# Strassen's method for both feed-forward products of a windowed attention block

## The chip, the cores and the metric

The kernel runs on one core of a Trainium2 chip. A core has five engines with queues of their own: TensorE (PE: matmuls, and PEld for their weight loads), VectorE (DVE), ScalarE (ACT), GpSimd (POOL) and SyncE (SP), which issues the DMAs here. Each engine works its queue in order. Matmuls write into PSUM (eight banks of 128 x 512 floats); everything else lies in SBUF. The metric is the device time of one execution in microseconds.

## The reference

```python
def _attn_ref(q, k, v):                      # q, k, v: 8 x 8 heads x 576 x 64
    scores = scale * np.matmul(q, k.transpose(0, 1, 3, 2))
    rel = pos[:, None] - pos[None, :]
    mask_plain = (rel >= 0) & (rel < 32)                           # heads 0 to 3
    mask_dil = (rel >= 0) & (rel < 128) & (rel % 4 == 0)           # heads 4 to 7
    scores = np.where(masks, scores, -1e9)
    attn = np.exp(scores - np.max(scores, axis=-1, keepdims=True))
    return np.matmul(attn / (np.sum(attn, axis=-1, keepdims=True) + 1e-09), v)

def _moe_ref(x, g_ln, w_ch1, w_ch2):         # x: 8 x 576 x 512, w_ch1: 512 x 2048
    mu, var = np.mean(x, -1, keepdims=True), np.mean((x - mu) ** 2, -1, keepdims=True)
    xn = (x - mu) / np.sqrt(var + 1e-06) * g_ln
    return x + np.maximum(xn @ w_ch1, 0.0) @ w_ch2
```

Attention with a window of 32 keys (plain or with a stride of 4), then a normalisation, a product with a 512 x 2048 weight, a relu, a product with a 2048 x 512 weight, and the residual sum. The rows, 8 x 576, are 36 tiles of 128.

## The kernel before

Each tile of 128 rows goes through the same stages. Its queries, keys and values are loaded (`L` in the program's table of units). TensorE makes the scores (`S`, L196) of the window in PSUM; VectorE adds the mask (L204) and takes the maximum (L213), GpSimd subtracts it (L225), ScalarE takes the exponential (L226), VectorE transposes (L228): `M`. TensorE multiplies with the values (`V`, L250), VectorE divides (L255 to L260) and four DMAs put the strided heads into the rows `x` (L267). `N` normalises: L274 to L278 on VectorE, the power on GpSimd (L279, `rstd`), `xn` on VectorE (L288). `xn` is then written as two float16 halves, the upper by a cast on ScalarE (`xh`, L293), the lower by a subtraction on GpSimd (`xl`, L294), and two transposing DMAs (`T`, L301) bring both into the layout that the matmuls need.

Both weights, too, are kept as two float16 halves, so that a float32 product is three float16 matmuls: upper with upper, upper with lower, lower with upper. In the first 100 us both weights are unpacked, scaled and split, mostly by VectorE (L386 to L391 and L137).

The feed-forward part works on blocks of three tiles. An "up" product takes 12 matmuls of 384 columns for each of 16 slices of 128 hidden units (L322); ScalarE writes the relu's upper half (`hh`, L328) and VectorE the lower one (`hl`, L329). A "down" product of one tile takes 48 matmuls of 512 columns (L345); VectorE scales it and adds `x` (L351), and a DMA writes the tile out. In the first two blocks, six tiles, the up products go tile by tile, with 128 columns.

The order of the work comes from a table of units with due times and predecessors; they are emitted in the order of these times, and a scheduler that keeps a timeline of its own then places every engine's instructions.

## Time and profile before

| | before |
|---|---|
| median of 3 runs | 926.09 us (924.34 to 927.63) |
| profiled execution: time, span | 925.45 us, 923.70 us |
| granted TensorE clock, mean | 0.985 |
| TensorE busy | 872.5 us, 94% |
| weight loads (PEld) busy | 518.8 us, 56% |
| VectorE busy | 364.3 us, 39% |
| ScalarE busy | 179.8 us, 19% |
| GpSimd busy | 102.3 us, 11% |
| DMA | 75.33 MB, mean 82 GB/s |

A row of instruction groups reads: line, engine, operation, output and inputs with their shapes, count | busy time in us, mean ns of one | idle time of the engine just before them, and who ended it. A row of the chain of waits reads: start, length in us, and what it was; the chain is followed back from the last instruction to whatever released each step. A row of the timeline reads: start, length, engine, line, operation, and in brackets the idle time before it. Matmuls are pipelined, so the length of one is longer than its share of a stream.

### The profile page before, as it was taken

To read this page: it belongs to the slowest core of one execution; us is meant where nothing else is said; L and a number is where in the kernel's file an instruction comes from. 1 tells how busy PE (TensorE), PEld (TensorE's weight loads), DVE (VectorE), ACT (ScalarE), POOL (GpSimd) and SP (SyncE) were. 2 spreads that over 40 slices of the span, in tenths; PEclk is the share of its full clock that TensorE was granted. 3 is DMA by queue.
4 is the path that set the end of the run, shared out by engine and by line. 5 is a ranking of instruction groups with operands and counts; after the bars stand their busy time and mean duration, and the time that the engine had idled before them with its cause. 6 is when DMAs were issued, how large, how long until landed. Compare 5 with 4: busy or idle time off the path is not lost.

```text
span 923.7 us, 27029 instructions
## 1 busy us (share of the span) xinstructions
PE 872.5 (94%) x12392; PEld 518.8 (56%) x12392; DVE 364.3 (39%) x727; ACT 179.8 (19%) x332; POOL 102.3 (11%) x125
## 2 busy tenths in 40 slices
PE   3459999999999999999999999999999999999998
PEld 2358575767554654654654554554554554554553
DVE  5998622334432432432432432432432432340220
ACT  4464410111210210210210210220220120120210
POOL 1011211111111111111101101101101111110000
PEclk9968999999999999999999999999999999999999
DMA  9963322432222221321312312322212212110000
GB/s 326 345 234 98 71 70 72 109 76 71 82 59 81 71 59 55 97 60 51 99 46 65 98 39 68 93 56 70 77 54 73 80 52 69 37 24 29 12 1 35
DMA packets 95154, 75.33 MB, mean 82 GB/s; under 512 B 44800, under 2 KB 77120, under 8 KB 95040
## 3 DMA queue, kind: packets, MB, share of 16 engines
q1 hardware_dynamic: 95040, 73.60, 27.0%
q8 instruction: 97, 1.59, 0.7%
q14 instruction: 17, 0.14, 0.0%
HBM read 49.97 MB, written 9.44 MB: 64 GB/s over the span
## 4 chain that ended last, share of the span: by engine, by line
PE 81%; SPq 2%; DVE 2%; DMA 1%; issue 1%; ACT 1%; POOL 0%; DVEq 0%; POOLq 0%; ACTq 0%
PE ps_f L345 38%; PE ps_f L322 36%; PE ps_v L250 4%; PE ps_s L196 3%; DMA x<-xd 1%; SPq L267 1%; SPq L301 1%; DVE bs L274 0%; SPq L158 0%; DVE hl L329 0%; ACT xh L293 0%; DVE xn L288 0%; ACT hh L328 0%; POOL rstd L279 0%; DVE row L351 0%
## 5 line engine op out<-in xcount | busy, mean ns | idle before, releaser
L345 PE MATMUL ps_f<-w_sb,hh 128*128 128x512 f16 x1152 | 343.0, 379 | 2.0 <-ACT hh L328 2.0
L322 PEld LDWEIGHTS <-w_sb 128*128 128x128 f16 x3072 | 255.8, 99 | 129.7 <-issue 2.8
L345 PE MATMUL ps_f<-w_sb,hl 128*128 128x512 f16 x576 | 218.3, 379 | 1.6 <-DVE hl L329 1.5
L322 PE MATMUL ps_f<-xT,w_sb 128*128 128x384 f16 (+1 forms) x1536 | 199.0, 292 | 14.9 <-DMA xT<-xh 12.6
L322 PE MATMUL ps_f<-w_sb 128*128 128x384 f16 (+1 forms) x1536 | 193.3, 286 | 0.0
L345 PEld LDWEIGHTS <-hh 128*128 128x128 f16 x1152 | 109.9, 98 | 130.4 <-ACT hh L328 2.3
L329 DVE SCALAR_TENSOR_TENSOR hl<-ps_f,hh 128x384 f16<-128x384 f32 (+1 forms) x184 | 104.7, 572 | 189.5 <-ACT hh L328 189.4
L328 ACT ACTIVATE hh<-ps_f 128x384 f16<-128x384 f32 (+1 forms) x184 | 91.6, 502 | 323.1 <-PE ps_f L322 323.1
L345 PEld LDWEIGHTS <-hl 128*128 128x128 f16 x576 | 56.4, 98 | 70.0 <-DVE hl L329 2.4
L279 POOL TENSOR_TENSOR rstd<-rstd,mhalf 128x1 f32<-128x1 f32 x36 | 21.8, 605 | 540.9 <-DVE rstd L278 530.3
L293 ACT CAST xh<-xn 128x512 f16<-128x512 f32 x36 | 22.2, 618 | 233.0 <-DVE xn L288 233.0
L351 DVE SCALAR_TENSOR_TENSOR row<-ps_f,s,x 128x512 f32<-128x512 f32 x36 | 27.0, 750 | 97.7 <-PE ps_f L345 97.7
L274 DVE BATCH_NORM_STATS2 bs<-x 128x6 f32<-128x512 f32 x36 | 24.9, 692 | 91.4 <-DMA x<-xd 91.4
L250 PE MATMUL ps_v<-vs,pt 32*32 32x65 f32 x3328 | 54.4, 228 | 0.0
L294 POOL TENSOR_TENSOR xl<-xn,xh 128x512 f16<-128x512 f32 x36 | 43.7, 1213 | 57.9 <-ACT xh L293 50.7
L250 PE MATMUL ps_v<-v_prev,pt 32*32 32x65 f32 x1152 | 48.4, 229 | 0.5 <-DVE pt L228 0.5
L225 POOL TENSOR_TENSOR sc<-sc,mx 128x512 f32<-128x512 f32 x32 | 34.3, 1072 | 122.6 <-DVE mx L213 109.2
L250 PEld LDWEIGHTS ps_v<-vs,pt 32*32 32x32 f32 x3328 | 46.4, 105 | 0.7 <-issue 0.7
L196 PE MATMUL ps_s<-ks,q 64*32 64x64 f32 (+1 forms) x2976 | 42.0, 218 | 3.6 <-issue 3.6
L196 PEld LDWEIGHTS ps_s<-ks,q 64*32 64x32 f32 x2976 | 34.6, 109 | 18.6 <-issue 18.1
L250 PEld LDWEIGHTS ps_v<-v_prev,pt 32*32 32x32 f32 x1152 | 38.0, 105 | 12.2 <-issue 11.0
L226 ACT ACTIVATE p<-sc 128x512 f32<-128x512 f32 x32 | 20.2, 630 | 116.3 <-POOL sc L225 116.3
(49 smaller groups left out, 313.1 us busy)
## 6 DMA issues: line engine op xcount, KB each, us to landing
slot<-in_w SPq DMA_DIRECT2D x14, 1024.0 KB, 7.7
ks<-in_qkv SPq DMA_DIRECT2D x36, 256.0 KB, 3.3
q<-in_qkv SPq DMA_DIRECT2D x36, 256.0 KB, 3.5
vs<-in_qkv SPq DMA_DIRECT2D x36, 256.0 KB, 3.8
out_x<-row SPq DMA_DIRECT2D x36, 256.0 KB, 2.0
x<-xd SPq DMA_DIRECT2D x144, 32.0 KB, 2.1
v_prev<-in_qkv SPq DMA_DIRECT2D x35, 128.0 KB, 3.0
slot<-in_w SPq DMA_DIRECT2D x4, 512.0 KB, 8.0
```

Source lines behind the costliest of these rows:

```text
L196: nc.tensor.matmul(sc[pj, b, h, cols], q[on, h, pj], keys, start=not early and n == 0, stop=not early and n == len(terms) - 1 or early and ...
L225: nc.gpsimd.tensor_tensor(out=sc, in0=sc, in1=mx.broadcast_to([P, 2, HP, 2 * W]), op=ALU.subtract)
L250: nc.tensor.matmul(pv[to, b, g, e], pt[pj, b, h, n], v[pj, f, e], start=n == 0 or b == 1 and old is None, stop=n == 1,)
L274: nc.vector.bn_stats(bs, x)
L279: nc.gpsimd.tensor_tensor(out=rstd, in0=rstd, in1=mhalf, op=ALU.pow)
L293: nc.scalar.copy(xh, xn)
L294: nc.gpsimd.tensor_tensor(out=xl, in0=xn, in1=xh, op=ALU.subtract)
L322: nc.tensor.matmul(z[:, n], l, r, start=(m == 0), stop=(m == len(mm) - 1))
L328: nc.scalar.activation(hh, z, AF.Relu)
L329: nc.vector.scalar_tensor_tensor(out=hl, in0=z, scalar=0.0, in1=hh, op0=ALU.max, op1=ALU.subtract)
L345: nc.tensor.matmul(o, l, r, start=(f == 0 and m == 0), stop=(f == NFC - 1 and m == 2))
L351: nc.vector.scalar_tensor_tensor(out=y, in0=o, scalar=state["inv"], in1=state[t]["x"], op0=ALU.mult, op1=ALU.add,)
```

## The change

Tiles 0 to 5 keep the plain products, now always tile by tile. From tile 6 on, tiles go in pairs, 256 rows. Both operands of a product are cut into quarters, and in place of eight products of quarters there are seven, on sums of quarters (the form with 15 additions). The first weight's columns and the second's rows are cut into two hidden halves of 1024 (`s` = 0 and 1), and each half of a pair has seven up products (`U`, 24 matmuls of 128 columns each, L418 of the new file) and seven down products (`D`, 12 matmuls of 256 columns each, L487). The constant `ORDER` lists one pair's work: `U04` is up, half 0, product 4; `N01` and `N05` are the next pair's `U01` and `U05`; `S0`, `S1`, `V0` and `V1` are scores and values of the first and second tile of pairs to come.

- Sums of the weights, `T1` to `T4` for each weight and each fourth of the hidden units, are made once and kept: `T1` and `T2` on GpSimd, `T3` and `T4` on VectorE, each with a cast on ScalarE (L390 to L400). `T4` overwrites a quarter and waits for the last plain product that reads it.
- `norm` of a pair's second tile makes four sums of quarters on GpSimd (L300) and then the halves of five quarters, 1280 columns, in one cast (L308) and one subtraction (L309); its two transposing DMAs carry 1280 columns. The transposed operand of a pair has one buffer.
- Partial sums stay in PSUM: products 1, 6, 7 and 4 accumulate in one bank, 5 and 3 in another, and between them the running sum is copied out (L435, ScalarE) or added up (L440, VectorE). Relu, four more sums of the hidden quarters (L445, VectorE), a cast on ScalarE (L426) and a subtraction on GpSimd (L427) make the halves of seven operands, `A11`, `A12`, `A22` and `S1` to `S4`, per hidden half.
- Each of the 14 down products of a pair is added into `x` in place (L498, VectorE), and `x` itself is written out.
- Scores and values share two PSUM banks; six are left for products.

```diff
-NB = 3
+FIRST = 6
+KQ = 256
...
-        xh = work.tile([P, DM], F16, name="xh")
-        xl = work.tile([P, DM], F16, name="xl")
-        nc.scalar.copy(xh, xn)
-        nc.gpsimd.tensor_tensor(out=xl, in0=xn, in1=xh, op=ALU.subtract)
...
+            for to, x0, x1, op in ((4, 2, 3, add), (5, 4, 0, sub), (1, 1, 5, sub), (2, 0, 2, sub)):
+                nc.gpsimd.tensor_tensor(out=xs[:, to], in0=xs[:, x0], in1=xs[:, x1], op=op)
+            st.update(halves_for_transpose(xs[:, 1:6], 1))
...
+    def combine(w, op, fg):
+        sub, add = ALU.subtract, ALU.add
+        x, y = {"T1": ("12", "11"), "T2": ("22", None), "T3": ("22", "12"), "T4": ("21", "T2")}[op]
+        e = nc.vector if op in ("T3", "T4") else nc.gpsimd
...
+    PRODUCTS = {
+        1: ("A11", "11"), 2: ("A12", "21"), 3: ("S4", "22"), 4: ("A22", "T4"), 5: ("S1", "T1"), 6: ("S2", "T2"),
+        7: ("S3", "T3"),
+    }
...
+    def up_product(n, s, to, start):
+        x, w = PRODUCTS[n]
+        q = QUARTER[x]
+        for j in range(HG):
+            fc = slice(j % 2 * P, (j % 2 + 1) * P)
+            ws = piece(0, w, 2 * s + j // 2)
+            for k in range(2):
+                for m, (l, r) in enumerate(triple([a[:, k, fc] for a in ws], (xT_pair[:, 0, q, k], xT_pair[:, 1, q, k]))):
+                    nc.tensor.matmul(
+                        to[:, j * P : (j + 1) * P], l, r, start=start and j == 0 and k == 0 and m == 0,
+                        stop=j == HG - 1 and k == 1 and m == 2, skip_group_check=not start,
+                    )
+
+    def halves(name, me, z):
+        h = me[name] = halves_tile()
+        hh, hl = flat(h)
+        nc.scalar.copy(hh, z)
+        nc.gpsimd.tensor_tensor(out=hl, in0=z, in1=hh, op=ALU.subtract)
+
+    def up(n, s, t0):
...
+        def added(x, z, name):
+            with tc.high_priority():
+                nc.vector.tensor_tensor(out=z, in0=x, in1=z, op=ALU.add)
+            nc.scalar.activation(z, z, AF.Relu)
+            halves(name, me, z)
+
+        def summed(to, x, y, op, name):
+            nc.vector.tensor_tensor(out=me[to], in0=me[x], in1=me[y], op=op)
+            halves(name, me, me[to])
...
+        else:
+            up_product(4, s, me["u"], False)
+            me["z21"] = f32_tile()
+            with tc.high_priority():
+                nc.scalar.activation(me["z21"], me["u"], AF.Relu)
+            me["s"] = f32_tile()
+            summed("s", "z21", "z22", ALU.add, "S1")
+            summed("z21", "z11", "z21", ALU.subtract, "S3")
+            summed("z11", "s", "z11", ALU.subtract, "S2")
+            summed("z12", "z12", "z11", ALU.subtract, "S4")
...
+        def to_x(i, half, ps):
+            x = state[t0 + i]["x"][:, half * KQ : (half + 1) * KQ]
+            with tc.high_priority():
                 nc.vector.scalar_tensor_tensor(
...
+                    out=x, in0=ps[:, 0:KQ], scalar=state["inv"], in1=x, op0=ALU.mult, op1=ALU.add
                 )
...
+        bank_of, adds = {
+            1: ("du", ((0, 0),)), 5: ("df", ((1, 1),)), 6: ("du", ((0, 1),)), 2: ("de", ((0, 0),)),
+            3: ("df", ((0, 1),)), 7: ("du", ((1, 1),)), 4: ("du", ((1, 0),)),
+        }[n]
...
+    ORDER = (
+        "U06", "U02", "V0", "U03", "U07", "S1", "U11", "U15", "U04", "U16", "U12", "U13", "U17", "D01", "D05", "V1", "U14", "D06",
+        "D02", "D03", "D07", "S0", "D11", "D15", "D04", "D16", "D12", "D13", "D17", "N01", "N05", "D14",
+    )
```

What the scheduler makes of it is seen in the engines' queues. GpSimd before, in the steady part, has three instructions a tile (`sc` is the subtraction before the exponential):

```order
L225 TENSOR_TENSOR sc<-sc,mx 128x512
L279 TENSOR_TENSOR rstd<-rstd,mhalf 128x1
L294 TENSOR_TENSOR xl<-xn,xh 128x512
L225 TENSOR_TENSOR sc<-sc,mx 128x512
L279 TENSOR_TENSOR rstd<-rstd,mhalf 128x1
```

and now, from the last lower half (`h`, L427) of the three made of products 2, 3 and 7 of half 0 to the second tile's `xl`:

```order
L427 TENSOR_TENSOR h<-z,h 128x512
L309 TENSOR_TENSOR xl_13664<-xs,xh_13663 128x512
L222 TENSOR_TENSOR sc<-sc,mx 128x512
L427 TENSOR_TENSOR h<-z,h 128x512 x11
L276 TENSOR_TENSOR rstd<-rstd,mhalf 128x1
L300 TENSOR_TENSOR xs<-xs 128x256 x4
L222 TENSOR_TENSOR sc<-sc,mx 128x512
L309 TENSOR_TENSOR xl_14078<-xs,xh_14077 128x1280
```

The second tile's `rstd` has moved behind eleven lower halves; in some pairs one of these comes behind it, and `sc` between the four sums.

VectorE at the same place, from the statistics of the second tile (L271) on, with `z` for sums of hidden quarters and `ps_f` for products:

```order
L271 BN_STATS bs_6841<-x_6761 128x6
L445 TENSOR_TENSOR z_6468<-z_6795,z_6468 128x512
L498 SCALAR_TENSOR_TENSOR x_5412<-ps_f_6660,s2_1703,x_5412 128x256
L273 BN_AGGR mv_6843<-bs_6841 128x2
L445 TENSOR_TENSOR z_6570<-z_6570,z_6468 128x512
L275 TENSOR_SCALAR rstd_6845<-mv_6843 128x1
L498 SCALAR_TENSOR_TENSOR x_5412<-ps_f_6827,s2_1703,x_5412 128x256
L498 SCALAR_TENSOR_TENSOR x_5412<-ps_f_6679,s2_1703,x_5412 128x256
L290 TENSOR_SCALAR xs_6437<-x_6761,mv_6843,rstd_6845 128x512
L498 SCALAR_TENSOR_TENSOR x_5848<-ps_f_6660,s2_1703,x_5848 128x256
L201 TENSOR_TENSOR sc_6920<-ps_a_6883,mask_16_75 128x512
L210 TENSOR_REDUCE mx_6938<-sc_6920 128x8
```

The normalising instruction (L290) waits for GpSimd's `rstd`, and additions into `x` and the next scores stand behind it. In the weight stage, VectorE's queue has sums of `T3` between the splits of the first weight (L133) and the unpacking of the second (L537):

```order
L133 SCALAR_TENSOR_TENSOR w_sb<-w_sb,gs 128x512 x2
L397 TENSOR_TENSOR z<-z,w_sb 128x512
L133 SCALAR_TENSOR_TENSOR w_sb<-w_sb,gs 128x512
L395 TENSOR_TENSOR z<-w_sb 128x512
L537 SCALAR_TENSOR_TENSOR w_sb<-w_sums 128x1024 x2
L257 TENSOR_TENSOR x<-ps_a,rs 128x256
```

where before only splits and unpacking stood; sixteen instructions of `T3` come before the second weight's scale.

More of the change, by code (lines that the diff above doesn't have):

```diff
@@ L167, in slot @@
     def slot():
-        return work.tile([P, CW * DM * 2], I32, name="slot", bufs=SLOTS)
+        n = state["raws"] = state.get("raws", -1) + 1
+        return w_sums[:, 1 + n % 5].rearrange("p c f -> p (c f)").bitcast(I32)
     def attn_scores(t):
@@ L213, in attn_softmax @@
         nc.vector.reduce_max(mx, sc, axis=AX.X)
[L214 removed]
+        p32 = work.tile([P, 2, HP, 2 * W], F32, name="sc") if t < EARLY else sc
         by = 1.0 / 8.0
@@ new lines, in transposes, with bank, triple @@
+    def transposes(t):
+        st = state[t]
+        for a, src in enumerate((st["xh"], st["xl"])):
+            if t < FIRST:
+                out_ = x_place(t)[:, a]
+            else:
+                i = (t - FIRST) % 2
+                out_ = xT_pair[:, a, 2 * i : 2 + 5 * i].rearrange("p q k n -> p (q k) n")
+            nc.sync.dma_start_transpose(out=out_, in_=src)
+    def bank():
+        return ps_f.tile([P, DM], F32, name="ps_f")
+    def triple(w, x):
+        (wh, wl), (xh, xl) = w, x
+        return (wh, xh), (wh, xl), (wl, xh)
@@ new lines, in piece @@
+    def piece(w, name, fg):
+        half = slice(0, 2) if name in ("11", "12") else slice(2, 4)
+        cols = slice(0, KQ) if name in ("11", "21") else slice(KQ, 2 * KQ)
+        if name[0] == "T":
+            n = int(name[1])
+            if n < 4:
+                return [sums_16[:, 3 * w + n - 1, fg, :, a] for a in range(2)]
+            half, cols = slice(0, 2), slice(KQ, 2 * KQ)
+        if w == 0:
+            return [w1_16[:, fg, half, a, cols] for a in range(2)]
+        return [w2_16[:, 4 * fg + half.start : 4 * fg + half.stop, a, cols] for a in range(2)]
@@ new lines, in down_product @@
+    def down_product(n, s, to, start, me):
+        x, w = PRODUCTS[n]
+        h = me[x]
+        for j in range(HG):
+            wh, wl = (a[:, j % 2] for a in piece(1, w, 2 * s + j // 2))
+            hh, hl = h[:, 0, j], h[:, 1, j]
+            for m, (l, r) in enumerate(((hh, wh), (hh, wl), (hl, wh))):
+                nc.tensor.matmul(
+                    to[:, 0:KQ], l, r, start=start and j == 0 and m == 0,
+                    stop=j == HG - 1 and m == 2, skip_group_check=not start,
+                )
@@ L370, in to_f32 @@
+        start = n in (1, 5, 2)
+        if start:
+            me[bank_of] = bank()
+        down_product(n, s, me[bank_of], start, me)
+        for i, half in adds:
+            to_x(i, half, me[bank_of])
+        if s == 1 and n in (3, 4):
+            t = t0 + (n == 4)
+            nc.sync.dma_start(out=out[t * P : (t + 1) * P, :], in_=state[t]["x"])
     def to_f32(src, dst, ps, weights, start, stop, first=False):
@@ L418, in prep_w1 @@
         fs = slice(fg * DM, (fg + 1) * DM)
-        wf = w1_sb[:, fg + 1]
-        ps = ps_f.tile([P, DM], F32, name="ps_f")
+        wf = w1_f32(fg)
+        ps = bank()
         for c in range(0, NKC, CW):
@@ L437, in load_w2 @@
         if f == 0:
-            state["w2_ps"] = ps_f.tile([P, DM], F32, name="ps_f")
+            state["w2_ps"] = bank()
         to_f32(
@@ new lines, in attention_then_ffn @@
+    base, at, step = start + 2 * TOOK["U"], {}, 0.0
+    for what in ORDER:
+        at[what] = step
+        step += TOOK[what[0]]
+    products = []
+    for t in range(FIRST, NT, 2):
+        now = base + step * ((t - FIRST) // 2)
+        for what in ORDER:
+            kind = what[0]
+            if kind in "UD":
+                products.append((now + at[what], kind, t, int(what[1]), int(what[2])))
+            elif kind == "N" and t + 2 < NT:
+                products.append((now + at[what], "U", t + 2, 0, int(what[2])))
@@ new lines, in attention_of_pair @@
+    def attention_of_pair(t0, last_up):
+        for i in range(2):
+            t, now = t0 + i, base + step * ((t0 - FIRST) // 2)
+            s, v = now - step * (2 - i) + at[f"S{i}"], now - step + at[f"V{i}"]
+            attention(t, s, s + SOFTMAX, v, v + NORM, v + NORM + READY, last_up)
+    attention_of_pair(FIRST, f"U{FIRST - 1}.3")
+    for n in (1, 5):
+        products.append((start + 0.3 * n, "U", FIRST, 0, n))
+    was = f"D{FIRST - 1}.3"
+    for when, kind, t, s, n in sorted(products):
+        after = (f"T{t + 1}", f"T4.0.{2 * s + 1}") if kind == "U" else (f"T4.1.{2 * s + 1}",)
+        name = f"{kind.lower()}{t}.{s}.{n}"
+        unit(name, when, lambda kind=kind, t=t, s=s, n=n: (up if kind == "U" else down)(n, s, t), was, *after)
+        was = name
+        if (kind, s, n) == ("U", 1, 4) and t + 2 < NT:
+            attention_of_pair(t + 2, name)
```

316 lines of the change are left out of this document (169 added, 147 removed).

## The prediction

> **What bounds the kernel now.** I read the page's busy shares and slices first, then the chain of waits in order of time.
>
> ```profile
> PE 872.5 (94%) x12392; PEld 518.8 (56%) x12392; DVE 364.3 (39%) x727; ACT 179.8 (19%) x332; POOL 102.3 (11%) x125
> PE   3459999999999999999999999999999999999998
> PEclk9968999999999999999999999999999999999999
> ```
> ```profile
> 162.45 2.68 PE ps_f L322 x48
> ...
> 441.29 3.90 PE ps_f L322 x24
> 445.19 1.41 PE ps_v L250 x91
> 446.60 9.86 PE ps_f L322 x60
> 456.46 0.90 PE ps_s L196 x34
> ...
> 481.71 1.16 PE ps_s L196 x70
> ...
> 505.21 0.85 PE ps_s L196 x32
> 506.07 5.29 PE ps_f L345 x24
> 511.35 3.90 PE ps_f L322 x24
> ...
> 826.65 31.08 PE ps_f L345 x144
> 857.73 31.20 PE ps_f L322 x192
> ```
> From about 260 us on, each piece of the chain is TensorE work that starts where the one before it ended. One block of three tiles takes 511.35 - 441.29 = 70.06 us, so a pair of tiles 46.71. The last block has no attention in it and prices the feed-forward work alone: 31.20 + 31.08 = 62.28 us a block, 41.52 a pair. Attention adds 1.41 (values) and on average 0.97 (scores) a tile, 4.76 a pair. Together 46.28; the missing 0.43 lies at the seams of attention pieces. What costs time here is TensorE's columns and nothing else. The first 100 us are another regime:
>
> ```profile
> 20.00:40.00 20.00, 11.36 (x342) 9.25 (x343) 19.64 (x30) 11.02 (x19) 0.00 (x0) 1.00 0.99 364
> 40.00:60.00 20.00, 5.90 (x79) 5.27 (x77) 20.00 (x42) 12.67 (x23) 4.14 (x2) 0.59 0.66 227
> 60.00:80.00 20.00, 18.97 (x349) 17.22 (x348) 20.00 (x33) 8.99 (x12) 2.83 (x2) 0.84 0.63 214
> ```
> The columns are stretch, PE, PEld, DVE, ACT and POOL busy, granted clock, DMA share, GB/s. There VectorE, busy without a gap on the weights, is the bound.
>
> **TensorE.** A pair now has 14 up and 14 down products in place of 16 and 16 quarter products: 24 matmuls of 128 columns or 12 of 256 each. 128 columns have rows: 48 took 2.68 us, 55.8 ns each, and
>
> ```profile
> 84.14 10.79 PE L322 MATMUL ps_f<-xT,w_sb 128*128 128x128 f16 x190
> ```
> gives 56.8 across changes of bank. 256 columns have none; 384 took 31.20/192 = 162.5 ns, so 256 lies between 56 and 163, and halfway in columns is 109.2 ns. An up product is then 1.34 us, a down product 1.31, and a pair 14 x 2.65 = 37.1 us; with the same 4.76 and 0.43 a pair is 42.29 us if nothing waits. The gain is 4.42 us a pair, 66.3 in 15 pairs.
>
> The rows speak against one rule here. The Trainium skill ("TensorE: Matmul & The Clock Gate", Back-to-back issue gap) says that a real stream of weight loads and matmuls sustains about 81 ns at 128 columns, and that the 56 ns are the isolated case. The 190 matmuls above are such a stream, each with its own load.
>
> **Other engines.** Rows by form:
>
> ```profile
> L204 DVE TENSOR_TENSOR sc<-ps_s,mask 128x512 f32<-128x512 f32 x32 | 21.9, 685 | 37.2 <-PE ps_s L196 37.2
> L288 DVE TENSOR_SCALAR xn<-x,mv,rstd 128x512 f32<-128x512 f32 x32 | 17.5, 546 | 14.5 <-POOL rstd L279 14.3
> L260 DVE TENSOR_TENSOR x<-ps_v,rs 128x256 f32<-128x256 f32 x36 | 15.2, 424 | 1.1
> L226 ACT ACTIVATE p<-sc 128x512 f32<-128x512 f32 x32 | 20.2, 630 | 116.3 <-POOL sc L225 116.3
> L293 ACT CAST xh<-xn 128x512 f16<-128x512 f32 x36 | 22.2, 618 | 233.0 <-DVE xn L288 233.0
> ```
> ```profile
> L294 POOL TENSOR_TENSOR xl<-xn,xh x36: 1151/1155/2022, 53.4 to 829.0; 128x512 f16<-128x512 f32 x36
> L225 POOL TENSOR_TENSOR sc<-sc,mx x32: 1041/1042/2012, 104.2 to 809.9; 128x512 f32<-128x512 f32 x32
> L279 POOL TENSOR_TENSOR rstd<-rstd,mhalf x36: 548/548/2122, 46.5 to 827.0; 128x1 f32<-128x1 f32 x36
> ```
> (The second view gives least, median and most ns.) Per pair GpSimd gets 14 lower halves at 1.155 = 16.2 us, four sums of 256 columns and one xl of 1280, beside two sc, two rstd and one xl as now: about 26 us in 42. ScalarE gets 28 pieces near 0.62, some 20 us in all, VectorE 6 additions from PSUM (0.685), 8 sums in SBUF and 14 additions into x (near 0.42), some 25 in all. No engine is full. What can fail is latency, and one resource is shared:
>
> ```profile
> 53.17 1.23 DVE L391 SCALAR_TENSOR_TENSOR w_sb<-slot 128x1024 int32<-128x1024 int32 x1
> ...
> 53.39 2.02 POOL L294 TENSOR_TENSOR xl<-xn,xh 128x512 f16<-128x512 f32 x1 [4.73 <-ACT xh L293]
> ```
> GpSimd's 1.155 us became 2.02 beside a VectorE instruction with two inputs in SBUF; 54.40, where VectorE ended, plus one undisturbed length is its end. Beside instructions with an input in PSUM the median stays 1.155. So the 8 sums of a pair and GpSimd's work take turns. The Trainium skill says the same as a rule ("SBUF — State Buffer", Who interferes with whom): an exclusive lock, held for the whole instruction. By it alone, no term below would differ.
>
> **The chain** that I expect to set the period: the next pair's second tile gets its attention values (V1) in this pair, and U05, the first up product that needs this tile, stands near the end. Today that way from values to transposed operand is short:
>
> ```profile
> 446.24 0.36 PE L250 MATMUL ps_v<-vs,pt 32*32 32x65 f32 x14
> ...
> 447.47 0.42 DVE L260 TENSOR_TENSOR xd<-ps_v,rs 128x256 f32<-128x256 f32 x1
> ...
> 451.72 0.69 DVE L274 BATCH_NORM_STATS2 bs<-x 128x6 f32<-128x512 f32 x1 [1.95 <-DMA x<-xd]
> ...
> 452.97 0.55 POOL L279 TENSOR_TENSOR rstd<-rstd,mhalf 128x1 f32<-128x1 f32 x1 [14.33 <-DVE rstd L278]
> ...
> 454.78 1.21 SPq L301 DMA_TRANSPOSE xT<-xh  x1
> ...
> 456.09 1.20 SPq L301 DMA_TRANSPOSE xT<-xl  x1
> 457.38 0.54 SPq L155 DMA_DIRECT2D ks<-in_qkv  x1
> ```
> ```profile
> xT<-xh SPq DMA_TRANSPOSE x18, 2.5
> ```
> V ends at 446.60; rstd starts 6.4 us later, and the last transpose lands near 12.
>
> In the new order, eleven lower halves stand ahead of this rstd on GpSimd (ten in some pairs). The first of them, of operand S1 of half 0, can start an estimated 4.5 us after U04 ends: ScalarE's exp of 0.63, which itself waits about 1.1 for its sc, then U04's relu 0.6, the sum 0.69, the cast 0.62, handovers, and one more sum's turn. U04 ends 9.4 us before V1 does (four up products, two down, V1). From there eleven halves are 12.7 us, and five sums of VectorE that take turns with them 3.0 (0.6 each, between 0.546 and 0.685): rstd starts 4.5 + 12.7 + 3.0 - 9.4 = 10.8 us after V1, not 6.4. Bounds: 8.2, if no sum is in the way (U14's eviction, 3.6 after V1, and four halves), and 12.4 with longer sums. Then, from V1's end, with bounds where there is no row:
> - rstd 0.55, xn 0.6: 11.95.
> - Four sums xs: 0.52 (half of L225) to 0.80 (half-way from L279's one column to L225's 512), I take 0.65, and sc between or behind them, 1.04: 15.6.
> - Cast of 1280: 1.0 to 1.55, taken 1.3: 16.9. The transpose of xh is issued here.
> - xl of 1280: 2.06 to 2.89, taken 2.5: 19.4.
> - Transpose of 1280 columns. Today's issue of 1.21 us may stay or grow 2.5 times, to 3.03; with a fixed part like the plain issue's (0.54 and less) it is 2.5. It lands 1.3 after its issue ends, as 2.5 against 1.21 shows. That of xl follows that of xh on SP: 19.4 + 2.5 + 1.3 = 23.2.
>
> Between the rest of U05 and V1's end TensorE has U05, U06, a part of U02, V0, nine more up products, two down, one tile's scores and V1, 21.65 us, so the period is 21.65 + 23.2 = 44.85 us, 2.56 more than 42.29. Summing the low ends gives 18.1 and no wait, the high ends 27.0 and a period of 48.6. Waits that arise on the way do not add: xn waits for rstd in VectorE's queue with additions into x behind it, and D07, D04 and D16 need those additions before they may go on in the same bank. TensorE stands a little there, and so the less at U05. The even tile's transposes have half a period to spare, ScalarE's copies 2.6 us of other products ahead of who needs them. The last pair brings nobody's attention: 14 waits, 35.8 us.
>
> **The head.** The 16 VectorE instructions of T3 of the first weights stand, by the new order, in the weight stage, where VectorE has no gap: 10.4 us at 0.65. A dozen of GpSimd's for T1 stand there too; each can hold up a two-input instruction by its 1.04, 12.5 us. Against that, matmuls of tiles 0 to 2 fill TensorE until 94.9 by the row at 84.14, and later small gaps can take some. Bounds 0 and 23; I take 12.
>
> **The sum,** against the profiled execution's 925.45 us (span 923.70; the median of the runs is 926.09, 0.6 more, which I leave aside): 925.45 - 66.3 + 35.8 + 12 = 907 us.
>
> **Rivals.**
> 1. *TensorE sets the period after all.* For: three terms of the chain were taken above their low ends, and 2.56 us are not much in 23. Against: the eleven halves are certain. Then 925.45 - 66.3 + 12 = 871.
> 2. *The chain eats the gain; slower.* Place: GpSimd's queue between U04 and xl of 1280. It decides from where the chain is (66.3 - 12)/14 = 3.9 us beyond 20.65 (= 42.29 - 21.65), that is 24.5 us after V1; I forecast 23.2. At 26, near the high ends, the wait is 5.35: 925.45 - 66.3 + 75 + 12 = 946. For: GpSimd doubled in the weight stage, and in-order queues rarely meet at the best moment. Against: the high ends would have to come together.
> 3. *128 columns cost more in the long run.* At 81 ns an up product is 1.94 us, a pair 8.5 us more, 50.8: 925.45 + 15 x 4.1 + 12 = 999. Against: both rows at 56.
> That fewer products run than written is excluded by the order: 24 and 12 matmuls a product, 28 products a pair.
>
> **How the numbers follow.** Forecast 0.43 (of it 0.04 within 0.3% of no change, 0.04 above), rival 1 0.20, rival 2 0.30 (0.03 of it within), rival 3 0.02; 0.05 for a head far off, divided evenly. A measurement of this kernel tells about 0.3%, some 3 us. Faster 0.57, same 0.08, slower 0.35. The range takes in nearly all of rival 2 and rival 1 at its upper part: 872 to 946. The forecast's own range, from the chain's terms moved by half their bounds, is 885 to 925.
>
> **What would show it.** If right, the pieces of the chain of waits between two L193 have a wait of TensorE at L418 for a transpose, 2 to 3 us in each pair, GpSimd is busy about 0.6 of the steady slices, and the first L418 comes some 12 us later than the same place now. Rival 1: TensorE has no wait in the steady part, period 42.3. Rival 2: period over 46. Rival 3: 24 matmuls over 1.6 us. Wrong altogether if the wait is for VectorE at a down product, or if xh's transpose lands before rstd's queue matters.

## The result and the profile after

The changed kernel takes 958.17 us (median of 4 runs, 955.79 to 961.86) against 926.86 (924.34 to 928.45) for the kernel before beside it: ratio 1.034, interval 1.030 to 1.039. It is slower; 907 was forecast. The profiled execution took 956.94 us, with a span of 955.1. Two of the kernels further down had one execution each at a lower granted clock (0.763 and 1084.6 us in experiment 3, 0.889 and 999.8 us in experiment 4), which their medians leave out.

Busy shares and slices of the changed kernel's page, as quoted of the kernel before:

```profile
PE 822.5 (86%) x16592; PEld 727.2 (76%) x16592; DVE 604.8 (63%) x1021; ACT 377.6 (40%) x624; POOL 522.1 (55%) x451
PE   3318799956999999989999899988999898898998
PEclk9999799977999999999999999999999999999999
```

TensorE does less in three places: in the weight stage, up to about 120 us (3, 3, 1, 8, 7 where 3, 4, 5, 9, 9 stood), from about 190 to 240 us, with a low clock there, and at single slices all through the pairs. The first two are the head. There the same table by stretches as in the prediction (length, then PE, PEld, DVE, ACT and POOL busy, granted clock, DMA share, GB/s); from 60 to 80 us TensorE was busy 18.97 us before:

```profile
60.00:80.00 20.00, 8.99 (x127) 8.82 (x127) 20.00 (x29) 7.90 (x12) 9.98 (x5) 1.00 0.08 16
...
180.00:200.00 20.00, 15.31 (x143) 9.76 (x140) 20.00 (x16) 3.62 (x6) 20.00 (x14) 0.95 0.19 35
200.00:220.00 20.00, 8.33 (x224) 8.01 (x224) 20.00 (x17) 5.59 (x10) 20.00 (x14) 0.67 0.11 34
220.00:240.00 20.00, 16.75 (x209) 9.34 (x212) 16.88 (x29) 2.47 (x5) 8.12 (x6) 0.79 0.15 41
```

From 180 to 220 us VectorE and GpSimd are busy without a gap, both, and TensorE is not. A look at both timelines there shows that they take turns. GpSimd:

```profile
185.63 1.60 POOL L397 TENSOR_TENSOR z<-z,w_sb 128x512 f32<-128x512 f32 x1
187.20 1.60 POOL L395 TENSOR_TENSOR z<-w_sb 128x512 f32<-128x512 f16 x1
```

VectorE:

```profile
179.88 1.65 DVE L395 TENSOR_TENSOR z<-w_sb 128x512 f32<-128x512 f16 x1
181.45 0.68 DVE L352 SCALAR_TENSOR_TENSOR z<-ps_f,z 128x512 f16<-128x512 f32 x1
182.05 2.60 DVE L396 TENSOR_TENSOR z<-z,w_sb 128x512 f32<-128x512 f32 x2
```

Each weight sum takes 1.6 us on GpSimd, step after step, because one of VectorE's stands ahead of it; while VectorE's sums wait, its instructions for the plain tiles (L352, L201) wait behind them in the same queue. The first up product of a pair starts at 260.5 us, 31.4 us later than the kernel before starts its first block of three (229.1):

```profile
L418 PE MATMUL ps_f<-xT,w_sb x24: 219/219/219, 260.5 to 261.8; 128*128 128x128 f16 x24
```

From there on a pair takes 46.4 us on average (start of one pair's first up product to that of the next; 14 of them, 41.4 to 51.7), not 44.85. The chain of waits at one seam between two pairs, in order of time (start, length, what):

```profile
475.18 2.71 POOL h L427 x2
477.90 0.52 POOL rstd L276
...
478.44 0.56 DVE xs L290
...
479.06 0.74 POOL xs L300
...
482.28 0.70 POOL xs L300
...
483.00 1.27 ACT xh L308
...
484.28 3.48 DMA xT<-xh
...
487.80 0.94 PE ps_f L418 x14
```

V1 ended near 467.3. The chain that was forecast is there, with its sizes: lower halves, `rstd`, `xn`, sums, cast, transpose, up product. TensorE's waits from 300 to 900 us (who waited, for what: us in all, times, longest):

```profile
PE ps_f L487 <- DVE x L498: 13.5, 11, 2.7
PE ps_f L418 <- DMA xT<-xl: 8.6, 5, 2.7
PE ps_f L418 <- DMA xT<-xh: 7.6, 8, 2.4
PE ps_f L418 <- ACT z L435: 3.4, 3, 1.9
```

Nearly as much time goes to down products that wait for an addition into `x` (13.5 us) as to transposes (16.2 us). All these down products (8.9 us at D07, 4.4 at D16, 0.3 at D17) stand between V1 and U05. All waits together are 41.4 us, 3.2 a pair.

### The profile page after: what moved, and what is told of

It is laid out like the page before. It is cut to its first block, busy times and chain, and to the rows that moved or that the text cites. A ratio compares the mean times of both kernels' runs of the same rounds, so it can differ in the third digit from the quotient of the medians.

```text
span 955.1 us, 36608 instructions
## 1 busy us (share of the span) xinstructions
PE 822.5 (86%) x16592; PEld 727.2 (76%) x16592; DVE 604.8 (63%) x1021; ACT 377.6 (40%) x624; POOL 522.1 (55%) x451
## 4 chain that ended last, share of the span: by engine, by line
PE 39%; DVE 17%; POOL 16%; issue 12%; DMA 11%; ACT 3%; SPq 3%; DVEq 0%; POOLq 0%; ACTq 0%
PE ps_f L418 18%; PE ps_f L487 10%; POOL h L427 8%; DMA xT<-xh 4%; DMA x<-xd 3%; PE ps_a L247 3%; PE ps_f L344 3%; DVE z L445 3%; PE ps_f L363 2%; SPq L264 2%; DVE w_sb L133 2%; DMA xT<-xl 2%; POOL xl L309 2%; POOL xs L300 2%; DVE w_sums L533 1%
## 5 line engine op out<-in xcount | busy, mean ns | idle before, releaser
L427 POOL TENSOR_TENSOR h<-z,h 128x512 f16<-128x512 f32 x210 | 273.2, 1325 | 211.1 <-ACT h L426 189.8
L487 PEld LDWEIGHTS <-h 128*128 128x128 f16 x2520 | 244.1, 98 | 46.8 <-issue 17.3
L418 PE MATMUL ps_f<-xT,w_sb 128*128 128x128 f16 x2880 | 185.1, 219 | 3.3 <-issue 1.6
L418 PEld LDWEIGHTS <-w_sb 128*128 128x128 f16 x2880 | 167.8, 98 | 18.6 <-issue 13.5
L487 PE MATMUL ps_f<-w_sb,h 128*128 128x256 f16 x1440 | 174.2, 274 | 0.6 <-DVE x L498 0.6
L426 ACT CAST h<-z 128x512 f16<-128x512 f32 x210 | 127.7, 618 | 93.0 <-DVE z L445 89.7
L418 PE MATMUL ps_f<-xT,w_sums 128*128 128x128 f16 x2160 | 138.3, 220 | 22.8 <-DMA xT<-xh 8.9
L498 DVE SCALAR_TENSOR_TENSOR x<-ps_f,s,x 128x256 f32<-128x256 f32 x210 | 94.6, 472 | 94.9 <-PE ps_f L487 94.4
L445 DVE TENSOR_TENSOR z<-z 128x512 f32<-128x512 f32 x120 | 134.1, 1118 | 21.4 <-ACT z L473 16.9
L487 PE MATMUL ps_f<-w_sums,h 128*128 128x256 f16 x1080 | 134.5, 275 | 14.9 <-DVE x L498 14.0
L418 PEld LDWEIGHTS <-w_sums 128*128 128x128 f16 x2160 | 126.7, 98 | 15.6 <-issue 15.2
L435 ACT COPY z<-ps_f 128x512 f32<-128x512 f32 x90 | 52.5, 585 | 142.9 <-PE ps_f L418 142.9
L440 DVE TENSOR_TENSOR z<-ps_f,z 128x512 f32<-128x512 f32 x90 | 60.5, 684 | 57.5 <-PE ps_f L418 56.1
L344 PE MATMUL ps_f<-xT,w_sb 128*128 128x128 f16 x1152 | 70.9, 226 | 23.1 <-DMA xT<-xh 18.4
L309 POOL TENSOR_TENSOR xl<-xs,xh 128x512 f16<-128x512 f32 (+1 forms) x36 | 67.1, 1863 | 38.2 <-ACT xh L308 33.3
L308 ACT CAST xh<-xs 128x512 f16<-128x512 f32 (+1 forms) x36 | 31.8, 884 | 76.6 <-DVE xs L290 36.2
L271 DVE BATCH_NORM_STATS2 bs<-x 128x6 f32<-128x512 f32 x36 | 24.9, 691 | 55.3 <-DMA x<-xd 54.6
L193 PE MATMUL ps_a<-ks,q 64*32 64x64 f32 (+1 forms) x2976 | 43.3, 220 | 16.7 <-issue 15.8
```

The costliest lines, as they stand in the source:

```text
L309: nc.gpsimd.tensor_tensor(out=xl[:, 0:m], in0=x, in1=xh[:, 0:m], op=ALU.subtract)
L344: nc.tensor.matmul(z[:, n * P : (n + 1) * P], l, r, start=n == 0 and c == 0 and m == 0, stop=n == HG - 1 and c == NKC - 1 and m == 2,)
L418: nc.tensor.matmul(to[:, j * P : (j + 1) * P], l, r, start=start and j == 0 and k == 0 and m == 0, stop=j == HG - 1 and k == 1 and m == 2, ...
L426: nc.scalar.copy(hh, z)
L427: nc.gpsimd.tensor_tensor(out=hl, in0=z, in1=hh, op=ALU.subtract)
L435: nc.scalar.copy(z, x)
```

## The experiments

All times are medians, ratios are against the kernel before on the same chip with the 95% interval; "period" is the mean distance of two pairs' first up products.

### 1. The head without sums

```diff
         (xh, xl) = piece(w, x, fg)
...
-        nc.scalar.copy(hi, z)
-        e.tensor_tensor(out=lo, in0=z, in1=hi, op=sub)
+        hi, lo = piece(w, op, fg)
+        nc.scalar.copy(hi, xh)
+        nc.scalar.copy(lo, xl)
```

> Left out: the sums of the weights. Each T1 to T4 is filled by two copies of an existing quarter on ScalarE, so VectorE and GpSimd have none of the 120 instructions L390 to L400; everything else is as in the changed kernel. Theory A (the sums, with VectorE and GpSimd in turns at 1.60 us each from 179 to 222 us, are what lengthened the head): the first up product in pairs, at 260.5 us now, comes near 230, granted clock 1.0 up to there, total 958 - 30 = about 927 us. Rival B (the new table, single tiles with 128 columns and the smaller pools lengthened it): the first up product stays at 250 or later, total 948 or more. The steady period should stay near 46.5 us by both.

This kernel leaves the sums out, so its products are not those of the method; it is there for its time. 919.23 us, ratio 0.991 (0.988 to 0.994). The first up product (L406 in this kernel) starts here:

```profile
L406 PE MATMUL ps_f<-xT,w_sb x24: 219/219/220, 227.5 to 228.8; 128*128 128x128 f16 x24
```

That is 33.0 us earlier than with sums, and the stretch that stood still works:

```profile
200.00:220.00 20.00, 20.00 (x425) 15.95 (x424) 7.31 (x15) 7.53 (x13) 3.37 (x5) 1.00 0.25 70
```

The period is 46.1. So nearly the whole loss of the head is the sums. The new table, the single tiles and the pools cost some 3 us: the first up product is 1.6 us earlier than the first block of the kernel before, but two values and two scores, near 5 us, are still to be done. Theory A stands, rival B falls. And the steady part is a second loss with a cause of its own.

### 2. All weight sums on VectorE

```diff
-        e = nc.vector if op in ("T3", "T4") else nc.gpsimd
+        e = nc.vector
```

> All 120 instructions of the weight sums on VectorE, none on GpSimd. Theory A, refined (the two engines exclude each other, so what counts is the sum of both lengths): 56 instructions of 1.04 to 1.15 us become 56 of about 0.65 us, 22 to 28 us less in the whole head, of which the stretch 179 to 222 us shrinks from 43 to about 35; the first up product comes at 240 to 252 us instead of 260.5, total 938 to 950. Rival (no exclusion; VectorE alone is too slow for twice the instructions): the first up product comes after 265, total over 962.

947.18 us, ratio 1.022 (1.018 to 1.025); the first up product comes at 245.4 us, 15.1 earlier. With twice the instructions VectorE is done sooner:

```profile
200.00:220.00 20.00, 18.40 (x207) 12.10 (x194) 20.00 (x36) 5.80 (x10) 0.00 (x0) 1.00 0.11 34
```

36 instructions in 20 us, 0.56 each, where the two engines together did 31 (17 and 14). By this, what counts is the sum of both engines' lengths, and a sum is shorter on VectorE. The first pair then took 56.7 us. No sum stands in it, the last one ends at 243.7 us. What comes late is its second tile: the statistics start at 252.3 us, and TensorE waits 6.2 us for the transpose of this tile's xh. So only 11 of the 15 us reach the total.

### 3. Fewer lower halves ahead of `rstd`

```diff
-        nc.gpsimd.tensor_tensor(out=hl, in0=z, in1=hh, op=ALU.subtract)
+        e = nc.vector if name[0] == "S" else nc.gpsimd
+        e.tensor_tensor(out=hl, in0=z, in1=hh, op=ALU.subtract)
```

> The lower halves of S1 to S4 (8 of GpSimd's 14 a pair) go to VectorE; rstd of the second tile then stands behind 3 lower halves rather than 11 or 10. Theory C (the chain V1, rstd, xs, xl, transpose sets the period): rstd starts about 6.5 us after V1 ends in place of 10.6, xl's transpose lands 4 us earlier, TensorE's wait ahead of U05 (1.85 us a pair) goes and the period falls from 46.4 to 43.5 - 44.5; total 925 to 935. Rival (waits in VectorE's queue, where additions into x stand behind sums, now with 8 more instructions of 0.6 to 0.75 us): the waits ahead of down products (1.7 us a pair) grow and the period stays at 46 or above; total 952 or more. The head stays at 260 by both.

955.75 us, ratio 1.030 (1.027 to 1.032): no gain. The same kernel was run once more for its profile.

> The kernel with the lower halves of S1 to S4 on VectorE once more, for a profile at full clock. Its time, 956 us, speaks against theory C (period 43.5 to 44.5): the rival now expects a period of 46 or more, no wait of TensorE for xl's transpose any more, and in its place more than 1.7 us a pair of waits of down products for VectorE's additions into x. If instead the granted clock is below 0.95 over the steady part, the time says nothing on the chain.

956.36 us (one execution), clock 0.978, period 46.4. The waits for transposes have not gone, against both expectations; they have grown from 16.2 to 23.9 us:

```profile
PE ps_f L418 <- DMA xT<-xh: 15.0, 11, 2.2
PE ps_f L418 <- DMA xT<-xl: 8.9, 8, 2.3
...
PE ps_f L488 <- DVE x L499: 4.7, 6, 2.3
```

The reason stands in VectorE's queue at one seam, where it began with V1's values at 752.83 and with the statistics (L271) at 758.71:

```profile
758.71 0.68 DVE L271 BATCH_NORM_STATS2 bs<-x 128x6 f32<-128x512 f32 x1
759.32 0.67 DVE L446 TENSOR_TENSOR z<-z 128x512 f32<-128x512 f32 x1
...
760.30 0.67 DVE L428 TENSOR_TENSOR h<-z,h 128x512 f16<-128x512 f32 x1
760.90 0.16 DVE L273 BATCH_NORM_AGGREGATE mv<-bs 128x2 f32<-128x6 f32 x1
...
761.36 0.67 DVE L428 TENSOR_TENSOR h<-z,h 128x512 f16<-128x512 f32 x1
761.96 0.14 DVE L275 TENSOR_SCALAR rstd<-mv 128x1 f32<-128x1 f32 x1
```

GpSimd had been empty for 7 us when `rstd` came:

```profile
762.18 0.55 POOL L276 TENSOR_TENSOR rstd<-rstd,mhalf 128x1 f32<-128x1 f32 x1 [7.13 <-DVE rstd L275]
```

Over the pairs `rstd` starts 11.2 us (median) after V1 ends, not 6.5, and later than with eleven halves ahead of it on GpSimd (10.2). The work that was taken from GpSimd's queue stands in VectorE's, between the three small steps of the same norm. So GpSimd's queue alone was not what held the chain.

### 4. V1 three products earlier

```diff
-        "U06", "U02", "V0", "U03", "U07", "S1", "U11", "U15", "U04", "U16", "U12", "U13", "U17", "D01", "D05", "V1", "U14", "D06",
+        "U06", "U02", "V0", "U03", "U07", "S1", "U11", "U15", "U04", "U16", "U12", "U13", "V1", "U17", "D01", "D05", "U14", "D06",
```

> One word of ORDER moved: V1 stands after U13 instead of after D05, three products (4.0 us) earlier; rstd of the second tile then stands behind 7 lower halves instead of 11 or 10. Theory C: the way from U04's end to the landing of xl's transpose is 4 to 5 us shorter, TensorE's wait ahead of U05 (1.85 us a pair) is gone, the other waits (2.6 us) stay: period about 44.5, total 958 - 14 x 1.9 = 931. Rival (the later halves, now behind rstd, xs and xl, make the down products D16, D12 and D13 wait instead): period 46 or above, total 952 or more.

976.67 us, ratio 1.054 (1.051 to 1.057), period 47.6: slower yet, by 18 us. The waits moved to where the rival put them:

```profile
PE ps_f L487 <- DVE x L498: 16.7, 19, 1.3
PE ps_f L487 <- POOL h L427: 12.6, 21, 1.6
```

Now the norm gets its turn earlier and the hidden operands get theirs later; 12.6 us are waits for lower halves, of which there were none.

### 5. More work ahead of U05

```diff
-        "U06", "U02", "V0", "U03", "U07", "S1", "U11", "U15", "U04", "U16", "U12", "U13", "U17", "D01", "D05", "V1", "U14", "D06",
-        "D02", "D03", "D07", "S0", "D11", "D15", "D04", "D16", "D12", "D13", "D17", "N01", "N05", "D14",
+        "U06", "V0", "U03", "U07", "S1", "U11", "U15", "U04", "U16", "U12", "U13", "U17", "D01", "D05", "V1", "U14", "D06",
+        "D02", "D03", "D07", "S0", "D11", "D15", "D04", "D16", "D12", "D13", "D17", "N01", "N02", "D14", "N05",
...
-    base, at, step = start + 2 * TOOK["U"], {}, 0.0
+    base, at, step = start + 3 * TOOK["U"], {}, 0.0
...
-    for n in (1, 5):
+    for n in (1, 2, 5):
```

> Two moves in ORDER and nothing else: the next pair's U02, which needs only the even tile, goes from behind U06 to ahead of U05, and D14 goes ahead of U05 too. 2.65 us of products more then stand ahead of the product that waits for the odd tile. Theory C (the chain through the odd tile sets the period, and the transposes' lateness is 1.85 us a pair on average, 2.7 at most): the wait of up products for transposes falls under 0.3 us a pair, period 44.6 - 45.0, total 958 - 14 x 1.8 = 933. Rival (the wait only moves: products behind U05 are short of 2.65 us of cover, so waits for ScalarE's copies and VectorE's additions grow by as much): period 46 or more, total 952 or more.

943.83 us, ratio 1.017 (1.014 to 1.021), period 45.5. About half of what theory C gives. Waits for xh's transpose are gone, those for xl's (8.7 us) stay, as do those of the down products (13.2, before 13.5):

```profile
PE ps_f L418 <- DMA xT<-xl: 8.7, 8, 2.2
```

### 6. The quarter sums on VectorE

```diff
-        nc.gpsimd.tensor_tensor(out=rstd, in0=rstd, in1=mhalf, op=ALU.pow)
+        with tc.high_priority():
+            nc.gpsimd.tensor_tensor(out=rstd, in0=rstd, in1=mhalf, op=ALU.pow)
...
-                nc.gpsimd.tensor_tensor(out=xs[:, to], in0=xs[:, x0], in1=xs[:, x1], op=op)
+                nc.vector.tensor_tensor(out=xs[:, to], in0=xs[:, x0], in1=xs[:, x1], op=op)
```

> The four sums of the odd tile's quarters (L300) on VectorE instead of GpSimd, where four took about 3.0 us; rstd is given priority, which leaves its place in GpSimd's queue as it is. Theory C: the sums take about 0.4 us each on VectorE (half of 685 ns and a little), the chain is 1.0 to 1.5 us shorter, the wait ahead of U05 falls by as much, period 45.2 - 45.7, total 938 to 945. Rival (VectorE's queue is what the down products wait for; four more instructions lengthen it): waits of down products over 1.7 us a pair, period 46.4 or more, total 955 or more.

958.16 us, ratio 1.032 (1.027 to 1.038), period 46.6; the four sums end 14.1 us after V1 ends, 0.9 earlier than before, and nothing is gained. The waits at down products (13.9 us) and for transposes (12.8 and 4.1, 16.9 together) are as they were.

### 7. Sums spread over two more plain tiles

```diff
-FIRST = 6
+FIRST = 8
-        e = nc.vector if op in ("T3", "T4") else nc.gpsimd
+        e = nc.vector
...
+        with tc.issue_after(state["split"]):
+            combine(w, op, fg)
...
-                    f"{op}.{w}.{fg}", TIMES["T"] + 36.0 * w + 8.0 * fg + 1.0 * n, lambda w=w, op=op, fg=fg: combine(w, op, fg),
+                    f"{op}.{w}.{fg}", TIMES["T"] + 60.0 * w + 15.0 * fg + 5.0 * n, lambda w=w, op=op, fg=fg: combine_later(w, op, fg),
```

`split` is the last split of a weight in VectorE's queue, so that no sum stands ahead of it; `T4` is due only near its first reader.

> Two tiles more in the plain form (8 instead of 6, 14 pairs instead of 15), all weight sums on VectorE, none before the last split of the weights, and their due times spread over the plain tiles. Two plain tiles take 46.7 us, a pair now takes 46.4, so this move costs nothing by itself. Theory A (the head is long because the sums crowd two engines that exclude each other): the first up product in pairs comes at 227.5 + 46.7 = 274 us to 280, the period stays 46.4, total 958 - 33 = 925, to 931. Rival (sums on VectorE hold up the plain tiles wherever they stand): the first up product after 290, total over 940.

938.30 us, ratio 1.012 (1.010 to 1.015). The first up product comes at 278.9 us, 4.9 after the 274 that would be no loss at all. The total lies over the 925 to 931 expected, since the first two pairs took 48.7 and 51.8 us with sums still in them. The edit gets back 20 of the 31 to 36 us that the head had lost; VectorE for all sums, without the spreading, had got back 11.

### 8. and 9. V1 far earlier

The order of one pair now reads

```python
"U06", "U03", "U07", "U11", "V1", "U15", "U04", "U16", "U12", "U13", "U17", "D01", "D05", "U14", "D06",
"D02", "D03", "D07", "S0", "D11", "D15", "D04", "D16", "D12", "D13", "S1", "D17", "N01", "V0", "N02", "D14", "N05",
```

With it go the steps by which scores and values are placed, and the first pair's U02.

> Only ORDER and the steps it is read at: the odd tile's values V1 come 11.7 us earlier (eight products and one tile's scores), V0 and the next pair's U02 go ahead of U05, both scores behind the down products of a period before. The last reader of the transposed operand, U14, then sets when xl's transpose may start, about 17 us of slack ahead of U05. Theory C': the period is set by whatever must follow V1 in VectorE's and GpSimd's queues, and 4 us (V1 three products earlier) only pushed that work onto the halves that D16 waits for, while 11.7 us put it where these queues are empty: TensorE waits for no transpose, the waits of down products stay at or below 1.7 us a pair, period 44.0 to 45.0, total 925 to 938. Rival (GpSimd's sums xs and xl between the lower halves, wherever V1 stands, make down products wait, as the 2.4 + 1.0 us of the earlier trial): period 46.4 or more, total 955 or more.

956.93 us, ratio 1.033 (1.028 to 1.037), period 46.2. TensorE waits for no transpose any more, and the time is the same to 0.2%. So the chain that I forecast is not what the time depends on by itself. What took its place:

```profile
PE ps_f L418 <- DVE z L440: 19.0, 9, 2.9
...
PE ps_f L487 <- DVE x L498: 4.5, 5, 2.6
```

L440 is the addition after an up product; U14 needs it to go on in the same bank. VectorE's timeline ahead of one such wait (470.3 to 472.9), with the addition that ends it (472.18), and the row of the group of the statistics:

```profile
459.23 0.42 DVE L257 TENSOR_TENSOR xd<-ps_a,rs 128x256 f32<-128x256 f32 x1
465.16 0.69 DVE L271 BATCH_NORM_STATS2 bs<-x 128x6 f32<-128x512 f32 x1 [5.51 <-DMA x<-xd]
465.76 0.67 DVE L445 TENSOR_TENSOR z<-z 128x512 f32<-128x512 f32 x1
...
472.18 0.68 DVE L440 TENSOR_TENSOR z<-ps_f,z 128x512 f32<-128x512 f32 x1
```
```profile
L271 DVE BATCH_NORM_STATS2 bs<-x 128x6 f32<-128x512 f32 x36 | 25.0, 694 | 111.6 <-DMA x<-xd 111.6
```

VectorE stood 5.5 us, with ready sums and additions behind it, because the statistics of a tile are first in its queue and wait for the four DMAs that bring the strided heads into `x`. Over the kernel that is 111.6 us, 3.1 a tile. In the changed kernel it is 55.3, as the scheduler happened to put sums ahead of these statistics; in the kernel before it is 91.4, where little stands behind.

> The far V1 together with the eight plain tiles and the weight sums spread on VectorE. If head and period are separate causes their gains add: 938.3 (sums spread alone) less 14 to 15 periods times what the far V1 gains in each. With a period of 44.5: 938 - 13 x 1.9 = 913, faster than the kernel before (926). If they are not separate (more VectorE work in the head of the pairs, or the clock), 930 or more.

941.78 us, ratio 1.018 (1.012 to 1.023): no faster than with the sums spread alone (938.30). This follows from the same: the far V1 gains nothing, with these sums or others.

### 10. and 11. The statistics behind other work

On top of the far V1:

```diff
+        with tc.issue_after(behind) if behind is not None else nullcontext():
+            nc.vector.bn_stats(bs, x)
```

where `behind` is an instruction of VectorE's queue, the addition of product 7, half 0, for the even tile and the sum S4, half 0, for the odd one. In the table of units, too, the tile's `N` comes after that product. No instruction is added or taken away.

> The far V1 of the trial before, and one more thing: the statistics of a tile (L271) are put behind other work in VectorE's queue, those of the even tile behind the addition of product 7 of half 0, those of the odd tile behind the sum S4 of half 0. In the trial before, VectorE stood 111.6 us ahead of L271, 3.1 us a tile, until the DMA x<-xd landed, with sums and additions behind it in its queue; TensorE waited for these additions ahead of U14 (19.0 us). Theory D (what sets the period is VectorE's in-order queue standing at the statistics): the wait ahead of L271 falls below 40 us, TensorE's wait for additions ahead of up products below 5 us in all, period 43.8 to 44.8, total 925 to 935. Rival (the two engines' turns on SBUF, or GpSimd's halves, set it): L271's wait falls, period stays at 46 or above, total 950 or more.

917.78 us, ratio 0.990 (0.988 to 0.992), period 43.5: 39 us less than with the far V1 alone, 1% faster than the kernel before, and better than the 925 to 935 expected. The group's row, TensorE's largest wait from 300 to 900 us, and its slices:

```profile
L274 DVE BATCH_NORM_STATS2 bs<-x 128x6 f32<-128x512 f32 x36 | 24.7, 687 | 24.2 <-DMA x<-xd 23.9
```
```profile
PE ps_f L421 <- issue: 8.0, 7, 2.4
...
PE   3317699974899899999999999999999999999998
```

TensorE's waits for VectorE are 0.2 us in all, and all its waits 14.4 us, where the far V1 alone had 40.3. Theory D stands.

> The same with eight plain tiles and the weight sums spread on VectorE. Theory D: 942 of that kernel without the moved statistics, less 13 periods of 2 us: 914 to 920, faster than the kernel before. Rival: 938 or more.

903.12 us, ratio 0.975 (0.973 to 0.977): 2.5% faster than the kernel before, and below the 914 to 920 expected, because a period fell by 3.05 us (47.15 to 44.10) and not by 2. Of the eleven pairs after the first two, seven take 42.5 to 43.3 us, which is the 42.29 of the forecast's TensorE term and little more; the others take 39.9 to 46.7. The gain that was forecast for TensorE is real; the change as it was made did not let it come out.

### 12. The statistics alone

The same edit with V1, V0 and U02 at their old places.

> The changed kernel with the statistics behind the same additions and sums as in the two trials before, but V1, V0 and U02 at their old places. Far V1 alone gave 957 us, both together 918. If the standing of VectorE at the statistics is the cause by itself: TensorE's waits fall as with both, period 44 to 45, total 925 to 938. If both are needed (near U05, the chain through the odd tile still ends last, since its statistics stand at the same place or later): waits for transposes of 1.5 us a pair or more stay, period 46 or above, total 950 or more.

957.47 us, ratio 1.032 (1.030 to 1.034). With this the four cases are complete:

| | statistics as they were | statistics behind |
|---|---|---|
| V1 as in the change | 958.2 | 957.5 |
| V1 far earlier | 956.9 | 917.8 |

Neither edit gains by itself, both together 40 us. At the old place the statistics stand behind sums in any case (their wait is 55.9 us with the edit, 55.3 without), so the edit alone changes next to nothing there, and the waits for transposes stay at 18.7 us. V1 close to U05 leaves no room for the norm to be late; V1 far away leaves that room, and the norm uses it only when it no longer stands first in a queue that others need.

### 13. The last sums on GpSimd

On the kernel of 903 us:

```diff
-        e = nc.vector
+        e = nc.gpsimd if (w, op) == (1, "T4") else nc.vector
```

> The fastest kernel so far (903 us) with the last sixteen weight sums, T4 of the second weight, on GpSimd in place of VectorE. There the first two pairs took 44.6 and 53.3 us against 42.8 later, with VectorE busy 19.97 and 16.71 of 20 us from 300 to 340 us and these sums in the chain of waits. If the number of VectorE's instructions there is the cause: the two periods come to 44 each, total 893 to 897. If the turns of the two engines are (each of these sums then stops both): no change or slower, 902 or more.

908.22 us, ratio 0.979 (0.976 to 0.981): 5 us more, though the two intervals touch. The first two pairs take 37.8 and 62.2 us in place of 44.6 and 53.3, not 44 each. The stretch with most of these sums, with all on VectorE:

```profile
300.00:320.00 20.00, 17.68 (x285) 15.33 (x283) 19.97 (x28) 9.47 (x16) 15.90 (x11) 0.91 0.19 41
```

and with sixteen on GpSimd:

```profile
300.00:320.00 20.00, 17.41 (x275) 14.87 (x272) 15.07 (x23) 8.36 (x15) 20.00 (x17) 1.00 0.19 42
```

VectorE has room now, but GpSimd has none (nor in the 20 us after), and the lower halves stand behind the sums in its queue. The load of one in-order queue was passed to another. The expectation named turns of the two engines as the rival; these rows show a full queue, which is not the same, so the turns are not shown to be the cause here.

## Why the prediction was wrong

**TensorE's term was right.** "A pair is 42.29 us if nothing waits": seven pairs of the kernel of 903 us take 42.5 to 43.3. The chain of waits of the kernel with far V1 and moved statistics has both kinds of product without a wait (start, length, what, count):

```profile
531.39 1.31 PE ps_f L494 x12
532.70 6.70 PE ps_f L421 x120
```

That is 55.8 ns for 128 columns and 109 for 256, each matmul with its own weight load, as estimated; rival 3 is out. By the Trainium skill's 81 ns ("TensorE: Matmul & The Clock Gate", Back-to-back issue gap) the 120 matmuls would take 9.7 us; the measurement decides against it for this stream.

**The step that failed in the head is the 92 sums that got no price.** The term was 12 us, measured about 36. The first up product came 31.4 us later, with two values and two scores, near 5 us of attention, still to be done. "The 16 VectorE instructions of T3 … stand in the weight stage" and "a dozen of GpSimd's" priced 28 of 120 instructions. Up to 180 us, where 47 stand, the loss was about these 12 us: from 20 to 180 us TensorE was busy 109.9 us with the sums and 122.0 with copies in their place. For what comes later the text has nothing but "later small gaps can take some". There were no gaps: from 180 to 240 us TensorE was busy 40.4 us, and 58.2 with copies. Each two of the sums took 1.6 us on one engine and 1.6 on the other, with plain tiles' work behind them in VectorE's queue. What was missing is a plain sum over all of `combine`: 56 times GpSimd's 1.04 and 64 times VectorE's 0.65, 100 us on two engines that take turns.

**The chain was right in size, and not alone.** Forecast after V1's end: `rstd` starts 10.8, sums end 15.6, cast ends 16.9. Medians of the trace: 10.2, 15.1, 16.3; at the seam shown, 10.6 and 17.0 for the first and last. GpSimd was 0.595 busy (357.2 of 600 us from 300 on), as written, and in each of 14 pairs it goes from a lower half to `rstd` without a gap. But a second way, nearly as long, stood beside the eleven halves: VectorE's own step of `rstd` (L275) ends 9.2 us (median) after V1, only 1.0 earlier, since sums and additions stand in its queue between statistics, aggregate and this step. The forecast had no term for it. So the third experiment, which moved halves from the one way into the other, gained nothing; `rstd` came at 11.2. The chain is a limit: 2.65 us more of cover took 14 us off the total. It is not the only one: when the far V1 took every wait for a transpose away, the period did not move.

**The step that failed in the steady part is the 21.65 us "between the rest of U05 and V1's end".** In 13 pairs of the changed kernel (all but the first and the last), from V1's end to the matmul of U05 that needs xl's transpose, the mean is 22.95 us, 23.2 forecast. TensorE waits 2.48 us on this way, 2.56 forecast, though over 1 us of it is not for a transpose but for additions into `x`. So "Waits that arise on the way do not add" held. From there to the next V1's end the mean is 23.84 us, 2.2 more than the forecast. TensorE waits 0.71 us a pair in it, at U16 for ScalarE's copies (3.0 us in all) and at other places, where the forecast had no wait. In five of the 13 pairs D14 and most of U02 stand behind U05, and not ahead of it as at the seam shown:

```profile
772.50 1.50 PE L418 MATMUL ps_f<-xT,w_sums 128*128 128x128 f16 x24
773.84 1.47 PE L487 MATMUL ps_f<-w_sb,h 128*128 128x256 f16 x12
```

These are U05 and then D14. The five take 25.8 us, the other eight 22.6; the forecast has one order for all pairs. These two things make some 1.6 of the 2.2 us; of the rest only 0.1 is seen, as half clock after a wait (below). The prediction had called itself wrong altogether "if the wait is for VectorE at a down product". This wait was there, 13.5 of 41.4 us, and the wait at L418 for a transpose was 1.25 us a pair, not 2 to 3. Behind it lies an assumption that the text did not say: that VectorE's queue, 59% busy from 300 to 900 us, gives each instruction its place when its data is ready. It stands at whatever is first.

**The sum again**, with what was measured: 907, + 24 for the head, + 21 for 14 periods of 46.36 in place of 44.85, + 5 in the last pair (42.2 to the last matmul in place of 37.5) gives 957 against the profiled 956.94. Two details of the forecast are off without effect: the high ends as listed add up to 26.6 us, not 27.0, and 54.40 plus 1.155 is 55.56, where the GpSimd row ends at 55.41.

**Rival 2** had the right side, slower, by the wrong mechanism: it put the point of decision at a chain of 24.5 us after V1, and the chain stayed under it, near 23. **Rival 1** is nearly what the pairs come to once the queues are mended.

What stays open: where the last half microsecond of the 2.2 goes, what the waits put down to "issue" are (8.0 us with the statistics behind), and why the last of the waits for xl's transpose stayed when U05 had 2.65 us more of cover.

## To carry over

Price every instruction that a change adds, one queue at a time, and where two engines exclude each other add their lengths before asking for gaps. An in-order queue is lost not by how busy it is but by what stands first in it and waits, so look in the groups' rows for idle time ahead of an instruction that waits for a DMA and ask what is ready behind it. Taking one obstacle away can gain nothing because the next one stands right behind it; when that only moves the wait, take it away together with the place to which it moved. Where a scheduler orders the work, read its order in every period before one period's sum is taken for all.
